# New orders of the same instructions in a fused chunked attention and snake-MLP kernel

## The chip, the cores and the metric

The kernel runs on one core of one Trainium2 chip. The metric is device time in microseconds (us), as the median of several executions. Before the change that median is 220.3 us, from three executions between 216.8 and 222.6 us. One further execution was taken by the hardware profiler; it took 214.84 us, and all times inside the kernel below come from it.

## The reference, cut to what matters

Four batches of 768 positions, eight heads of 64 channels. First a chunked attention: each chunk of 32 queries sees 16 keys to its left, its own 32, 8 to its right, and 8 memory keys. The result, 3072 rows of 512 channels, goes through a two-layer MLP of width 2048 whose activation is snake.

```
for c in range(nc):                       # 24 chunks of 32 positions
    k_full = concat(mem_k, k[c_start-16 : c_end+8])
    scores = scale * q_c @ k_full.T       # scale = 1/8
    a = softmax(scores)
    attn[c] = a @ v_full
x = attn.transpose(0, 2, 1, 3).reshape(3072, 512)
h = x @ w_in                              # 512 -> 2048
s = sin(alpha * h)
g = h + s * s / alpha
out = g @ w_out                           # 2048 -> 512, f32
```

## The kernel before, in words

The work is cut by batch. A stage runs the MLP of one batch (768 rows) on TensorE, and beside it the attention of the next batch. A front (stage -1) computes only the attention of batch 0, so five lists of words exist: the front, and passes 0, 1, 2 and 3. The last pass has no attention beside it.

Nothing is planned by a scheduler. Each list is an order written out by hand, and each word issues a few instructions. The engines run asynchronously, but each engine executes its own instructions in the order of the words; so a word moved in the list is moved on every engine and every queue that it issues to. The words, with their lines in the code:

- a (cast of a q or k piece to bf16, L653), k and l (12 TensorE transposes of a k or q piece, L274), K and L (the copy out of PSUM; for K a second small copy of the ends always on VectorE: L285, L291, L299). A trailing A means ScalarE, V means VectorE, P means GpSimd. Pieces a0 to a3 are k of head pair 0 to 3, a4 to a7 are q.
- s (scores, then exp on ScalarE: L317 to L332 for batch 0, L385 to L399 for the others), v (attention times values, L344 or L414, then the division on VectorE, L353 and L354, into a block of x).
- The block has to be turned into xT before the MLP can read it. T and t do it by four TensorE transposes (L366) and a copy out of PSUM (L369) by ScalarE or VectorE. c does it by a transposing DMA through the crossbar (L633), issued from the SP queue, with no compute engine in it.
- V (values by two or three DMAs from GpSimd's queue, L168 to L179), dm (the memory values, one DMA, L665), m (their copy into the value tile by VectorE, L188), I and U (the weights), R (rows of k and q of a coming batch, by GpSimd's queue), X (crossbar transposes of those rows, by the SP queue), Z (memory rows, SP queue), dk and dq (a whole batch of k or q).
- b and h (first layer of one of 16 feature tiles, first and second half, 4 matmuls each of 384 columns, L424; h also issues the Sin on ScalarE, L439), q (the square of the sine, L444 on ScalarE or L447 on VectorE or GpSimd), g (the sum into gT on VectorE, L451, which frees the tile's pair of PSUM banks).
- o and f (o opens the second layer of the pass, f takes n of its 96 matmuls, L462; finished rows are copied out at L469 and stored by the SP queue). In the last pass all 96 run behind the list.
- z (matmuls on zeros, L686), W (a dummy activation that brings in ScalarE's table for Exp or Sin, L699), e (which engine copies output rows), C (constants), H and Z (memory rows).

PSUM has eight banks. A feature tile holds a pair from its b to its g, a score or a value product holds a pair until it is read, and the open output rows hold one bank each. So at most four tiles are in flight, and TensorE waits at a b whose pair is not yet free. The order of the banks, of the x blocks and of the probability tiles is also decided by the order of the words.

Inputs of batch 0 come by eight DMAs from the SP queue (L708), in the order k0, q0, k1, q1, k2, q2, k3, q3.

Of the kernel before, what the change touches and what calls it, by code (L numbers as in the profile page):

```python
# [85 lines left out]
def kernel(  # L86
# [716 lines left out]
    def const_s():  # L803
# [7 lines left out]
    stage = Stage(-1, None)  # L811
    stage.tile = first
    stage.run((
# [3 lines left out]
    ))  # L817
    for i, words in enumerate(((
# [6 lines left out]
    ),(  # L825
# [5 lines left out]
    ),(  # L831
# [5 lines left out]
    ),(  # L837
# [3 lines left out]
    ))):  # L841
        stage = Stage(i, stage.nx).run(words)
    feed.take(400)
# [29 lines left out]
```

## Time and profile before

| What | us |
|---|---|
| median of three executions | 220.3 (216.8 to 222.6) |
| the profiled execution | 214.84 |
| its span, first to last instruction | 213.1 |
| TensorE (PE) busy | 201.7 (95%) |
| ScalarE (ACT) busy | 143.5 (67%) |
| VectorE (DVE) busy | 140.5 (66%) |
| GpSimd (POOL) busy, its DMA issues included | 99.8 (47%) |
| first layer, 512 matmuls (L424) | 86.0 |
| second layer, 400 matmuls (L462) | 89.1 |
| squares: ACT x30, DVE x23, POOL x11, mean of one | 0.84, 0.95, 1.58 |

A matmul is pipelined and its end is modelled, so TensorE counted as busy is not TensorE at its peak. Idle time of an engine costs something only where it holds up the engine that ends last. The chain that ended last runs 71% over PE, 9% over DVE, 7% over DMA, 4% over ACT and 3% over POOL. The granted clock of TensorE was 1.000.

### The profile page before, as it was taken

Reading aid. Unit: us, or ns where it says so; the run is one execution under the profiler, and the core shown is the slowest. Engines: PE = TensorE matmul, PEld = TensorE weight load, DVE = VectorE, ACT = ScalarE, POOL = GpSimd, SP = SyncE. Lnnn points to the kernel's source line nnn. Section 1 sums busy time; section 2 is a strip of 40 time slices with the busy share of each in tenths; the row PEclk is TensorE's granted clock in tenths of the full one; section 3 lists DMA queues with packets and bytes.
Section 4 is the critical chain, followed back from the end, with each engine's and each line's share of the span. In section 5 each row is a group of like instructions: output and inputs, shape, how many; then the busy total and the mean of one; then the engine's idle time right before and its main releaser. Section 6 shows DMA issues by size and latency. Waiting matters only on the chain.

```text
span 213.1 us, 4479 instructions
## 1 busy us (share of the span) xinstructions
PE 201.7 (95%) x1721; PEld 113.5 (53%) x1721; DVE 140.5 (66%) x218; ACT 143.5 (67%) x230; POOL 99.8 (47%) x140
## 2 busy tenths in 40 slices
PE   0799899999999999999999999999999999999994
PEld 0456555565455556555455555554555555554443
DVE  7598678999542749975856649898157197865011
ACT  2597898976857469977846199887846289891110
POOL 8959515688598193009991039659400023200000
PEclk9999999999999999999999999999999999999999
DMA  6999999999999999969999229989945400000312
GB/s 195 337 163 141 193 209 205 204 163 182 131 177 141 137 148 144 180 88 110 126 217 171 72 63 131 156 126 129 175 115 123 124 15 0 2 3 0 148 49 98
DMA packets 95908, 28.19 MB, mean 132 GB/s; under 512 B 84864, under 2 KB 92432, under 8 KB 95888
## 3 DMA queue, kind: packets, MB, share of 16 engines
q0 software_dynamic: 68736, 13.25, 92.3%
q1 hardware_dynamic: 26976, 14.62, 28.2%
q8 instruction: 13, 0.21, 0.4%
q14 instruction: 7, 0.06, 0.1%
q10 hardware_dynamic: 176, 0.04, 0.1%
HBM read 29.66 MB, written 6.29 MB: 169 GB/s over the span
## 4 chain that ended last, share of the span: by engine, by line
PE 71%; DVE 9%; DMA 7%; ACT 4%; issue 4%; POOL 3%; DVEq 0%; POOLq 0%; ACTq 0%
PE ps L462 38%; PE ps L424 27%; DMA memv_st<-in_mem_v_dram 4%; DVE gT L451 4%; DVE s L447 3%; DMA vw<-in_v_dram 3%; PE ps L414 3%; PE ps L385 2%; ACT u L439 2%; PE ps L366 1%; ACT s L444 1%; POOL s L447 1%; POOL vw L172 1%; DVE kT L285 1%; ACT L699 1%
## 5 line engine op out<-in xcount | busy, mean ns | idle before, releaser
L462 PE MATMUL ps<-w_out_sb,gT 128*128 128x512 bf16 (+2 forms) x400 | 89.1, 371 | 0.0
L424 PE MATMUL ps<-xT,w_in_sb 128*128 128x384 bf16 x512 | 86.0, 326 | 0.7 <-DVE gT L451 0.4
L451 DVE SCALAR_TENSOR_TENSOR gT<-s,inv_alpha,ps 128x768 bf16<-128x768 f32 x64 | 63.0, 1011 | 12.5 <-ACT s L444 5.2
L424 PEld LDWEIGHTS <-w_in_sb 128*128 128x128 bf16 x512 | 49.8, 98 | 35.4 <-issue 2.1
L439 ACT ACTIVATE u<-ps,alpha_sb 128x768 f32<-128x768 f32 x64 | 56.6, 895 | 16.8 <-PE ps L424 14.3
L462 PEld LDWEIGHTS <-gT 128*128 128x128 bf16 x400 | 36.6, 98 | 37.9 <-DVE gT L451 0.2
L447 POOL TENSOR_TENSOR s<-u 128x768 f32<-128x768 f32 x11 | 17.4, 1582 | 69.7 <-ACT u L439 69.7
L399 ACT ACTIVATE pt<-ps,biasm 128x256 bf16<-128x256 f32 x72 | 27.2, 489 | 10.5 <-PE ps L385 10.5
L469 DVE COPY o_sb<-ps 128x512 f32<-128x512 f32 (+1 forms) x15 | 10.1, 678 | 28.3 <-PE ps L462 26.4
L447 DVE TENSOR_TENSOR s<-u 128x768 f32<-128x768 f32 x23 | 21.9, 953 | 7.8 <-ACT u L439 7.8
L444 ACT ACTIVATE s<-u 128x768 f32<-128x768 f32 x30 | 25.0, 841 | 0.5
L354 DVE TENSOR_TENSOR x_blk<-ps,rinv 96x512 bf16<-96x512 f32 x32 | 22.0, 687 | 1.1
L469 ACT COPY o_sb<-ps 128x512 f32<-128x512 f32 (+1 forms) x10 | 5.6, 562 | 21.6 <-PE ps L462 21.6
L172 POOL DMA_DIRECT2D vw<-in_v_dram x13 | 12.9, 994 | 7.9 <-PE ps L366 5.4
L353 DVE RECIPROCAL rinv<-ps 96x8 f32<-96x8 f32 x32 | 6.4, 200 | 13.5 <-PE ps L414 12.7
L179 POOL DMA_DIRECT2D vw<-in_v_dram x13 | 12.7, 976 | 0.0
L238 POOL DMA_DIRECT2D kst<-in_k_dram x16 | 12.2, 760 | 1.1 <-DMA vw<-in_v_dram 0.8
L232 POOL DMA_DIRECT2D kst<-in_k_dram x16 | 11.3, 708 | 2.3 <-DMA vw<-in_v_dram 1.6
L369 ACT COPY xT<-ps 128x384 bf16<-128x384 bf16 x12 | 5.6, 496 | 8.2 <-PE ps L366 8.2
L245 POOL DMA_DIRECT2D q_bf<-in_q_dram x12 | 10.7, 912 | 0.0
L414 PEld LDWEIGHTS <-pt 128*128 128x128 bf16 x192 | 8.2, 97 | 4.2 <-ACT pt L399 0.3
L414 PE MATMUL ps<-vw,pt 128*128 128x65 bf16 x192 | 8.9, 193 | 0.0
(81 smaller groups left out, 131.4 us busy)
## 6 DMA issues: line engine op xcount, KB each, us to landing
out_dram<-o_sb SPq DMA_DIRECT2D x23, 256.0 KB, 2.3
kq_f<-in_k_dram SPq DMA_DIRECT2D x4, 384.0 KB, 6.5
kq_f<-in_q_dram SPq DMA_DIRECT2D x4, 384.0 KB, 6.0
q_bf<-in_q_dram POOLq DMA_DIRECT2D x12, 128.0 KB, 6.7
w_in_sb<-in_moe_w_in_dram POOLq DMA_DIRECT2D x1, 1152.0 KB, 12.6
vw<-in_v_dram POOLq DMA_DIRECT2D x7, 128.0 KB, 6.7
vw<-in_v_dram POOLq DMA_DIRECT2D x8, 112.0 KB, 7.4
kst<-in_k_dram POOLq DMA_DIRECT2D x14, 64.0 KB, 5.1
```

Of the source, the lines that this page charges most:

```text
L172: nc.gpsimd.dma_start(vw[0:64, lo:c1, 0:D], win(vflat, a, n, 64))
L179: nc.gpsimd.dma_start(vw[72:128, c0:hi, 0:D], win(vflat, base + QW * c0 + 48, hi - c0, 56))
L354: nc.vector.tensor_tensor(out=x_blk[:].rearrange("p g e d -> p e g d"), in0=otv[0:QW, :, :, 0:D], in1=rinv[:].unsqueeze(3).to_broadcast([Q ...
L399: nc.scalar.activation(pt[:, 0:H * QW].rearrange("p (g e c) -> p g e c", g=2, e=4)[:, :, :, 32 * m:32 * m + 32], sc[:, :, 0:4 * QW].rearra ...
L414: nc.tensor.matmul(otv[:, e, hp, :], pt[:, QW * i:QW * i + P], vws[b % 2][:, 2 * hp + e, j, 0:D + 1],)
L424: nc.tensor.matmul(t["hT"][:, hf, 0:HALF], w_in_sb[:, kt, P * t["ft"]:P * t["ft"] + P], t["xT"][:, kt, HALF * hf:HALF * hf + HALF], start= ...
L439: nc.scalar.activation(t["u"][:], t["hT"][:, :, 0:HALF], ACTF.Sin, scale=alpha_sb[:, ft:ft + 1])
L444: nc.scalar.activation(s2[:], u[:], ACTF.Square)
L447: e.tensor_tensor(out=s2[:], in0=u[:], in1=u[:], op=ALU.mult)
L451: nc.vector.scalar_tensor_tensor(out=gT[:, ft, :].rearrange("p (e c) -> p e c", e=2), in0=t["s2"][:], scalar=inv_alpha[:, ft:ft + 1], in1= ...
L462: nc.tensor.matmul(o[:, c0:c1], gT[:, ft, P * s:P * s + P], w_out_sb[:, ft, c0:c1], start=(ft == 0), stop=(ft == FT - 1),)
L469: copier(state["engines"][state["o"] % len(state["engines"])])(o_sb[:, c0:c1], o[:, c0:c1])
```

## The change

All five lists are written in another order. The number of instructions stays nearly the same; what changes in kind is this:

- Front: of the casts, a4 and a6 go from VectorE to ScalarE; of the copies out of PSUM, L1 goes to ScalarE, K1 to VectorE and K2 to ScalarE; two turned x blocks (30 and 31) go from ScalarE to VectorE. dm moves behind V024 in GpSimd's queue. The first four zero matmuls stand at the head. The first score word comes behind L1, a6 and K2 instead of ahead of a3.
- Pass 0: the square of tile 14 goes from VectorE to GpSimd, with V102 moved behind it; blocks 1 and 7 are copied by VectorE instead of ScalarE; block 3 goes through the crossbar and block 4 by TensorE instead of the other way round.
- Pass 1: the square of tile 7 goes from VectorE to GpSimd, that of tile 14 from ScalarE to VectorE; blocks 0 and 1 go through the crossbar instead of TensorE (five crossbar blocks instead of three); 5 and 6 exchange their copying engines. The dummy Exp comes behind the first scores.
- Pass 2: order only.
- Pass 3: the square of tile 14 goes from ScalarE to GpSimd.

The removed (-) and added (+) lines of the front and of passes 0, 1 and 3, cut to these places:

```diff
-        'a1A Cb Cp Cz Cv a5A eVA Cm Cl z4 a0V Ci k0 dm a4V l0 k1 K0V Ck l1 L0A V024 We L1V a2A K1A V002 '
-        'a6V k2 s00 K2V a3V s11 V068 m0 a7V s01 l2 s10 k3 K3A L2A V046 z4 v10 l3 Cs L3A I02 v11 s20 z1 '
-        'v01 s30 z1 v00 s31 z1 v30 s21 v31 T01 T10 v20 T30 T00 v21 T20 T31 I27 t11 t21 eVA Ws '
+        'Cz Cb a1A z4 a0V eVA Cp Cl k0 a4A a5A Cv Ck Ci l0 L0A K0V Cm l1 V024 a2A dm k1 V002 We k2 L1A K1V '
+        'a6A K2A a3V V068 s01 l2 m0 s00 a7V s10 s11 k3 K3A z4 L2A l3 L3A v10 Cs V046 v11 I02 z1 s30 v00 s20 '
+        'v01 s31 v30 s21 z1 T10 v31 z1 t30 T01 v20 v21 T00 t11 T20 t31 Ws eVA I27 t21 '
...
-        'o8 b0 h0 I7g q0V U69 U12 b1 h1 dq108 q1A b4 h4 b3 g0 h3 b6 g1 dk108 q4V g4 q3A b2 h2 h6 b5 h5 '
+        'b0 h0 o8 q0V I7g b1 U12 h1 U69 q1A dq108 g0 b4 dk108 h4 g1 b3 h3 b6 b2 q4V g4 q3A U56 h2 h6 b5 h5 '
...
-        'q15V h12 q12A b14 g15 f7 h14 V125 k1 k0 g12 l1 K1V k3 L1V L3A q14V K3A K0A V102 f9 g14 s61 f16 '
-        'm1 s70 s3 f13 v0 f3 v6 c6 f6 v3 f5 s542 T3 f10 T0 v4 f6 v2 f2 v1 c4 c2 f7 v7 f1 T1 f3 v5 Ws T7 '
-        'f8 t5 '
+        'q12A b14 f5 h14 g12 V125 k1 k0 l1 k3 K1V L1V L3A f2 q14P K3A K0A f9 g14 s61 f16 V102 s70 s3 m1 f13 '
+        'v0 f2 v3 f6 c3 v6 c6 f5 s542 f10 T0 v4 f8 v1 t4 v2 c2 v7 f7 t1 Ws f4 v5 f8 t7 f1 t5 '
...
-        'h15 f7 eV We s24 q15V f6 g15 f7 V268 s05 s1 f1 m2 f14 v4 v1 f6 v0 f1 v2 f2 c4 f6 s63 s7 t1 f4 c2 '
-        'v6 V357 T0 f4 v3 f4 v7 c7 v5 t3 f17 t5 T6 '
+        'q11A g7 f10 Ws b12 h12 g10 g11 q12P b14 g12 h14 b13 h13 q13A V202 q14V f7 X6 g13 b15 h15 f7 g14 s24 '
+        'q15V eV g15 f13 m2 s1 We V268 s05 f15 v4 v0 c4 v1 f6 v2 c2 f9 s63 s7 c1 f4 v6 V357 f4 v3 f4 v7 c0 v5 '
+        'c7 f3 t3 f14 t6 T5 '
...
-        'g12 b13 h13 b14 q15A h14 g15 q14A q13V g14 g13 '
+        'b14 g12 q13V q15A h14 q14P g13 g14 g15 '
```

23 rows, old and new, of the table stage are left out of this document.

## The prediction

> **What bounds the kernel now.** I read the page's busy shares first, then the busy time of each stage, then the front in order of time, then the chain.
>
> ```profile
> PE 201.7 (95%) x1721; PEld 113.5 (53%) x1721; DVE 140.5 (66%) x218; ACT 143.5 (67%) x230; POOL 99.8 (47%) x140
> PE   0799899999999999999999999999999999999994
> ```
>
> TensorE is nearly always busy, but not in the first slices. The table by stage (columns: length, then busy time of each engine with its instructions) has the front, passes 0, 1, 2, and pass 3 with the tail:
>
> ```profile
> 0.00:24.80 24.80, 17.19 (x289) 11.45 (x290) 19.54 (x54) 15.80 (x24) 21.00 (x50) 1.00 1.82 206
> 24.80:75.60 50.80, 50.30 (x473) 28.68 (x471) 35.53 (x52) 38.34 (x64) 30.79 (x38) 1.00 1.60 174
> 75.60:121.90 46.30, 46.29 (x370) 25.45 (x368) 33.34 (x47) 32.51 (x57) 22.18 (x27) 1.00 1.57 139
> 121.90:168.30 46.40, 46.24 (x362) 25.26 (x359) 30.18 (x42) 34.04 (x57) 21.37 (x23) 1.00 1.15 123
> 168.30:213.10 44.80, 41.72 (x240) 22.71 (x238) 21.88 (x24) 22.83 (x30) 4.44 (x3) 1.00 0.13 48
> ```
>
> From 24.8 us on TensorE is the bound: it idles 0.50, 0.01 and 0.16 us in three passes. Short waits hide in matmuls whose ends are modelled, so I also took the starts: a first-layer matmul follows the last after 162 ns at the median, a second-layer one after 216. All spacings over their line's median by more than 60 ns, without the roughly 0.1 us paid at each change to the 64-row score matmuls and back, add up to 2.9 us behind 24.8 us. That is all a better order can win in four passes, beside instructions that vanish. The front is the other place: 24.8 us in which TensorE waits for others.
>
> ```profile
> 7.30 0.83 ACT L653 CAST k_bf<-kq_f 128x768 bf16<-128x768 f32 x1 [3.87 <-DMA kq_f<-in_k_dram]
> 12.31 3.04 ACT L332 ACTIVATE pt<-ps 128x768 bf16<-128x768 f32 x4 [0.45 <-PE ps L325]
> 14.45 1.22 DVE L188 COPY vw<-memv_st 8x4096 bf16<-8x4096 bf16 x1
> 17.09 0.80 ACT L299 COPY qT<-ps 128x768 bf16<-128x768 bf16 x1 [0.43 <-PE ps L274]
> 24.81 11.91 PE L424 MATMUL ps<-xT,w_in_sb 128*128 128x384 bf16 x69
> 26.45 0.88 ACT L439 ACTIVATE u<-ps,alpha_sb 128x768 f32<-128x768 f32 x1
> ```
>
> ScalarE starts at 7.30, when k1 lands; its first four exps run from 12.31, its last q copy ends at 17.89, the MLP begins at 24.81 and the first Sin at 26.45. The chain shows what else stands there (start, length):
>
> ```profile
> 4.86 9.20 DMA memv_st<-in_mem_v_dram
> ...
> 14.34 1.75 POOL vw L172
> 16.09 6.06 DMA vw<-in_v_dram
> ```
>
> GpSimd's loads land in the order of issue, about 9 us behind it while the input loads are under way: memv from 4.86 at 14.06, V024 from 5.75 and 6.57 at 14.97 and 15.97.
>
> **The front, step by step.** In the new order ScalarE does, from 7.30: a1, a4, a5 (0.83 each), L0 (0.80), a2, the dummy (0.20), L1, a6 and K2 (0.70) before any exp. a4's input has landed at 5.8 (1.26 plus 4.5), yet it queues behind a1. 7.30 + 5 x 0.83 + 2 x 0.80 + 0.20 + 0.70 = 13.95: the first exp is 1.6 us later than 12.31. Four exps of 0.81, then K3, L2, L3 (0.70 + 2 x 0.80) end at 19.5, against 17.89. The next scores need L3: 0.65 on TensorE, then four exps of 0.81, about 23.5, against 21.99.
>
> VectorE loses a4, a6, L1 and K2 and gains K1 and two block copies, 1.5 us less work by their rows. But dm is now the third of GpSimd's loads: issued about 6.7, it lands near 15.9, where the third landed before (15.97), instead of 14.06. m0 waits for it on VectorE, with a7 and the ends of K3 queued behind it, and everything after a7 (l3, L3, v10) for those. m0 ends at 17.2 (before 15.67); a7 (0.6) 17.8; l3 stands ahead of v10 on TensorE, so the first division starts near 19.0 (before 16.56). Six more divisions of 0.89 lie ahead of block 20's end with one block copy of 0.4: 19.0 + 7 x 0.89 + 0.4 = 25.6. Its transposes (0.35) and T20 (0.43) give the first b at 26.4. Had memv landed in time, v31's exp would hold block 20 to about 25.2 and b to 26.0. t21 ends near 27.5, against 25.4, and h0 needs it. So the front costs **+1.6 us**, bounds +0.6 (divisions never queue, the two block copies taken from ScalarE pay) and +2.3 (Sin 28.5 against 26.45, with its table load behind T20). Nothing in pass 0 absorbs it: the weights it needs land at 26.72 and 32.17 and are not waited for.
>
> The zero matmuls now run near 1 us instead of 6.28, followed by idle until the alpha rows land at 5.96. Before, the four took 1.89 us, and 12 transposes 0.85 at 8.10 but 0.53 from 10.7 on.
> The Trainium skill, TensorE: Matmul & The Clock Gate, Part 1, says that the array runs at half rate until about 3.4 us of sustained work and falls back after an idle window as long. The halving agrees with these rows; by it the early zeros would be wasted and one more set of turns cold, 0.3 us, an estimate, and the front +1.9 instead of +1.6.
>
> **Pass 0.** Its end is where VectorE is late:
>
> ```profile
> 52.18 0.95 DVE L447 TENSOR_TENSOR s<-u 128x768 f32<-128x768 f32 x1
> 53.04 0.41 DVE L291 COPY kT<-ps 128x96 bf16<-128x96 bf16 x2
> 53.52 0.51 PE L385 MATMUL ps<-qT,kT 64*128 64x96 bf16 x16 [0.20 <-DVE kT L291]
> ```
>
> The 0.95 us square of tile 14 stands ahead of the key ends that the first scores wait for. On GpSimd it takes 1.46 to 2.03; V125 is issued by 49.3, so it can run from 50.7, and g14 is due about 4.8 us behind h14 against 0.9 + 1.8 + 1.0. The wait (0.36 from the starts) goes: **-0.4**, bounds -0.8 (with the three smaller waits of 44 to 51) and +0.5 (square and division late). V102 and the row loads move back by up to 3.2 us; its heads landed at 58.7 for a use at 61.1, and the row loads had 5.4 us of idle behind them. Late by more, v0 is next.
>
> **Pass 1.** Two blocks fewer on TensorE: 8 transposes at 42 ns start to start, **-0.3**. The copies (0.5 and 0.35) lie beside 0.216 us matmuls of the second layer. q7 on GpSimd: its loads ahead are issued by 81.7, it is free till 96.06, and it spares VectorE 0.95 off the path. The added crossbar blocks share SP's queue:
>
> ```profile
> 110.55 1.50 SPq L633 DMA_TRANSPOSE xT<-x_blk  x1
> 114.05 5.99 SPq L633 DMA_TRANSPOSE xT<-x_blk  x2
> ```
>
> One is 1.2 to 1.5 us in SP's queue and landed after 2.3 us (from 118.86) or 6.1 (from 110.55, among GpSimd's loads). Two more fit before block 7's if each takes the short time: c0 near 119, c7 near 120.2, landed by 122.5; b3 starts at 122.1 and h0 at 123.4. I take 0; the bound is +3.0, the long landing (120.2 + 6.1 = 126.3 against 123.4). The other bound is 0: that landing is not waited for now. The dummy Exp behind the scores puts 1.28 of table load ahead of the exps; 13 matmuls (2.8 us) cover it.
>
> **Passes 2 and 3** keep their work. Their waits were 1.1 us by the starts; an order can remove or double them, so 0, bounds -1.1 and +1.1. In pass 3, g14 is needed 28 second-layer matmuls (6.0 us) behind h14, and 0.9 + 1.8 + 2.0 fits; without this cover 1.0 us of the slower square would show.
> In the new lists three squares more go to GpSimd; at 133.73 one took 2.03 us beside VectorE's own square, at 126.04 1.46 almost without.
> The Trainium skill, GPSIMD Engine Reference, its specification table, says that GpSimd contends with VectorE instructions that read two SBUF inputs. The rows agree (VectorE's square stays 0.95); by it each new square costs 0.6 more at most, all covered, and the sum stays.
>
> **Sum.** +1.6 - 0.4 - 0.3 = +0.9: 215.7 us for the profiled execution's 214.84 (span 213.1, 1.7 around it). The median of the runs shown lies 5.5 above that execution, so **221.2 us** stands for the median, 220.3 + 0.9.
>
> **Rivals.**
> - *The passes win, the front is neutral.* Half of the 2.9 us of waits and the transposes: -1.8, 218.5. For it: ScalarE was busy 14.5 of the 17.5 us between 7.3 and 24.8 (15.80 less the 1.28 table load before), gaps which a denser order can use. Against it: the first exp waits for five casts and copies more. Chance 0.22.
> - *Slower: the crossbar blocks of pass 1 land late.* c0 or c7 behind V357's loads takes 6.1 us instead of 2.3, and TensorE stands before h0 of pass 2 for 3.0 us; with the front 1.6, +4.6: 224.9. It decides once c7 lands after 123.4 in the old clock. For it: 6.1 and 6.3 us landings at 110.55 and 98.86. Against it: 2.3 at 118.86, when those loads were through. Chance 0.13.
> - *It does nothing that counts.* TensorE runs the same matmuls, and the loads, not the casts, set the front (V046 landed 22.15, TensorE waited 0.25 for it): 220.3. Chance 0.10.
>
> **How the numbers follow.** Forecast 0.55 (its bounds: +0.6 - 0.8 - 0.3 - 1.1 = -1.6 and +2.3 + 0.5 - 0.3 + 1.1 = +3.6, or 218.7 to 223.9). 2%, 4.4 us, is about what a measurement of this kernel can tell from no change; three runs alone lay 5.8 apart. Slower by over 2%: the crossbar case nearly whole and a few hundredths of the forecast's upper end, 0.14. Faster by over 2%: no sum reaches it, since 2.9 + 0.3 is the limit of the passes; 0.06 for a front that gains on top. The rest 0.80. The range takes in 218.5 less the spread of medians, and 224.9.
>
> **What would show it.** First exp near 14.0 and first L424 near 26.4; L188 starting near 16 with a wait on memv_st; at the first L385 of pass 0 no wait on kT; L366 x64 instead of x72 and L633's xT x16; no wait on xT at the turn to pass 2. Wrong, if the first b comes by 24.8, or if TensorE's waits behind the front change by more than 2 us.

## The result and the profile after

The new orders cost time: 218.22 us is the median of 20 executions (216.3 to 220.8), against 215.48 us for 20 of the kernel before, a ratio of **1.0113 [1.0083, 1.0143]**, about 2.4 us. That is inside the 2% that the prediction called no difference, but it is a loss, and nearly three times the +0.9 us of the forecast. The three executions shown at first (216.8, 220.3, 222.6) lay high, so 220.3 was a poor base: 218.22 lies below the forecast's bounds of 218.7 to 223.9, and the same bounds counted from 215.48 are 213.9 to 219.1. Ratios, not medians, are compared from here on.

The profiled execution of the changed kernel took 219.58 us (span 217.4). It is one of 4 in 20 with a granted clock of 0.991 or 0.992 over the span (those four took 218.7 to 220.8 us); in its trace the clock is at half for 3.4 us of the front, so the trace shows more loss (4.7 us) than the median does. The page's busy line, TensorE's slices and its granted clock:

```profile
PE 201.9 (93%) x1694; PEld 114.5 (53%) x1713; DVE 138.8 (64%) x218; ACT 141.6 (65%) x225; POOL 104.7 (48%) x143
PE   3495989999999999999999999999999999999994
PEclk9998899999999999999999999999999999999999
```

TensorE is busy as long as before (201.9 against 201.7 us) in a span 4.3 us longer, and the idle slices are the first ones. The same table by stage as before (front, passes 0, 1, 2, then pass 3 with the tail):

```profile
0.00:29.08 29.08, 18.78 (x287) 12.76 (x290) 18.03 (x52) 17.41 (x26) 21.08 (x51) 0.94 1.58 193
29.08:80.00 50.92, 50.10 (x470) 28.81 (x473) 35.69 (x55) 36.94 (x60) 32.80 (x40) 1.00 1.59 160
80.00:126.00 46.00, 45.62 (x359) 25.10 (x363) 32.84 (x47) 31.18 (x55) 23.48 (x27) 1.00 1.59 149
126.00:172.60 46.60, 46.08 (x354) 25.35 (x356) 30.46 (x43) 34.05 (x57) 21.43 (x23) 1.00 1.22 122
172.60:217.40 44.80, 41.32 (x237) 22.47 (x236) 21.80 (x24) 22.02 (x29) 5.91 (x4) 1.00 0.12 46
```

The front is 29.08 us instead of 24.80: TensorE waits 10.30 us in it instead of 7.61, and is busy for 18.78 instead of 17.19, at a granted clock of 0.94. Cut at the first L424 of each pass, the four passes take 50.54, 46.36, 46.16 and 20.97 us (to the last L424 of pass 3); before 50.67, 46.58, 46.08 and 21.01. So they are 0.31 us shorter together. From the start of the last matmul to the end of the span it is 3.44 us, before 3.05. 4.27 - 0.31 + 0.39 = 4.35 us is the span's difference. The front in order of time (start, length, engine, line, and in brackets the wait and what ended it):

```profile
7.97 0.83 ACT L653 CAST k_bf<-kq_f 128x768 bf16<-128x768 f32 x1 [4.55 <-DMA kq_f<-in_k_dram]
...
14.03 2.87 ACT L332 ACTIVATE pt<-ps 128x768 bf16<-128x768 f32 x4
...
17.35 1.22 DVE L188 COPY vw<-memv_st 8x4096 bf16<-8x4096 bf16 x1 [2.46 <-DMA memv_st<-in_mem_v_dram]
18.60 0.75 DVE L653 CAST q_bf<-kq_f 128x768 bf16<-128x768 f32 x1
...
19.40 0.73 PE L274 MATMUL ps<-ident,q_bf 128*64 128x128 bf16 x12 [2.59 <-DVE q_bf L653]
...
20.73 0.20 DVE L353 RECIPROCAL rinv<-ps 96x8 f32<-96x8 f32 x1 [1.22 <-PE ps L344]
...
23.42 2.41 ACT L332 ACTIVATE pt<-ps 128x768 bf16<-128x768 f32 x3 [0.26 <-PE ps L325]
...
29.08 5.20 PE L424 MATMUL ps<-xT,w_in_sb 128*128 128x384 bf16 x31
...
30.58 0.90 ACT L439 ACTIVATE u<-ps,alpha_sb 128x768 f32<-128x768 f32 x1 [0.30 <-PE ps L424]
```

One queue after another is to be seen here. VectorE stands 2.46 us at m0 (L188) for the memory values; a7, the cast of the last q piece, stands behind it and ends at 19.35; TensorE stands 2.59 us at l3 for a7, with the first value product behind. Before, m0 ran at 14.45 with no wait. From l3 the chain to the first L424 runs through the copy L3 and the scores to the last three exps, which end at 25.83, and then through three divisions (L353, L354). k1 landed 0.67 us later in this execution (7.97 against 7.30); in the other traces it lands between 6.77 and 8.70, by chance. The chain has the load itself (start, length):

```profile
7.05 10.27 DMA memv_st<-in_mem_v_dram
```

Here 32 KB need 10.27 us, where the prediction took 9.2. The Trainium skill, DMA: Bandwidth & Descriptors, Anatomy of one DMA (the GpSimd path), gives a fit of 2.0 us plus bytes over 436,000 per us for one such DMA, an estimate of 2.1 us for this one; the trace does not agree with it under this load. That the loads ahead in the queue and the input loads beside it make the difference is argued from the order of the landings.

### The profile page after: what moved, and what is told of

Read it like the earlier page. It is cut to its first block, busy times and chain, and to the rows that moved or that the text cites. A ratio compares the mean times of both kernels' runs of the same rounds, so it can differ in the third digit from the quotient of the medians.

```text
span 217.4 us, 4445 instructions
## 1 busy us (share of the span) xinstructions
PE 201.9 (93%) x1694; PEld 114.5 (53%) x1713; DVE 138.8 (64%) x218; ACT 141.6 (65%) x225; POOL 104.7 (48%) x143
## 4 chain that ended last, share of the span: by engine, by line
PE 74%; DVE 10%; DMA 5%; ACT 4%; issue 4%; POOL 3%; DVEq 0%; POOLq 0%
PE ps L462 38%; PE ps L424 27%; DVE gT L451 5%; DMA memv_st<-in_mem_v_dram 5%; PE ps L414 3%; DVE s L447 2%; PE ps L385 2%; ACT u L439 1%; ACT s L444 1%; ACT pt L332 1%; PE ps L274 1%; DVE x_blk L354 1%; PE ps L366 1%; PE ps L344 1%; DVE vw L188 1%
## 5 line engine op out<-in xcount | busy, mean ns | idle before, releaser
L462 PE MATMUL ps<-w_out_sb,gT 128*128 128x512 bf16 (+2 forms) x383 | 87.0, 370 | 1.2 <-issue 0.5
L424 PE MATMUL ps<-xT,w_in_sb 128*128 128x384 bf16 x512 | 86.0, 326 | 0.8 <-DVE gT L451 0.5
L424 PEld LDWEIGHTS <-w_in_sb 128*128 128x128 bf16 x512 | 49.8, 98 | 35.4 <-issue 2.0
L447 POOL TENSOR_TENSOR s<-u 128x768 f32<-128x768 f32 x14 | 21.7, 1551 | 79.0 <-ACT u L439 42.7
L447 DVE TENSOR_TENSOR s<-u 128x768 f32<-128x768 f32 x22 | 21.0, 957 | 8.8 <-ACT u L439 8.8
L444 ACT ACTIVATE s<-u 128x768 f32<-128x768 f32 x28 | 23.5, 841 | 0.7
L354 DVE TENSOR_TENSOR x_blk<-ps,rinv 96x512 bf16<-96x512 f32 x32 | 22.0, 687 | 1.1
L353 DVE RECIPROCAL rinv<-ps 96x8 f32<-96x8 f32 x32 | 6.3, 198 | 15.6 <-PE ps L414 13.5
L232 POOL DMA_DIRECT2D kst<-in_k_dram x16 | 12.8, 798 | 0.0
L238 POOL DMA_DIRECT2D kst<-in_k_dram x16 | 11.6, 727 | 0.0
L245 POOL DMA_DIRECT2D q_bf<-in_q_dram x12 | 10.8, 914 | 0.0
L274 PE MATMUL ps<-ident,q_bf 128*64 128x128 bf16 x96 | 4.8, 252 | 4.8 <-DVE q_bf L653 2.6
```

The costliest lines, as they stand in the source:

```text
L232: nc.gpsimd.dma_start(kst[r0:64, j, :].rearrange("p (h d) -> p h d", d=D), k[b, :, lo + r0:lo + 64, :].rearrange("h p d -> p h d"),)
L354: nc.vector.tensor_tensor(out=x_blk[:].rearrange("p g e d -> p e g d"), in0=otv[0:QW, :, :, 0:D], in1=rinv[:].unsqueeze(3).to_broadcast([Q ...
L424: nc.tensor.matmul(t["hT"][:, hf, 0:HALF], w_in_sb[:, kt, P * t["ft"]:P * t["ft"] + P], t["xT"][:, kt, HALF * hf:HALF * hf + HALF], start= ...
L444: nc.scalar.activation(s2[:], u[:], ACTF.Square)
L447: e.tensor_tensor(out=s2[:], in0=u[:], in1=u[:], op=ALU.mult)
L462: nc.tensor.matmul(o[:, c0:c1], gT[:, ft, P * s:P * s + P], w_out_sb[:, ft, c0:c1], start=(ft == 0), stop=(ft == FT - 1),)
```

## The experiments

In the tables "front" is the first L424 less the landing of k1, which takes the luck of the input load out; before it is 17.5 us, after 21.1. One trace has some 0.5 us of chance in this (the seven traces with the front of before, those of before, e2, e11 and e15 to e18, lie between 16.8 and 17.8), so a ratio, where there is one, decides.

### One half each

e1 has the front of after and the passes of before; e2 the front of before and the passes of after.

```diff
-        'a1A Cb Cp Cz Cv a5A eVA Cm Cl z4 a0V Ci k0 dm a4V l0 k1 K0V Ck l1 L0A V024 We L1V a2A K1A V002 '
...
+        'Cz Cb a1A z4 a0V eVA Cp Cl k0 a4A a5A Cv Ck Ci l0 L0A K0V Cm l1 V024 a2A dm k1 V002 We k2 L1A K1V '
...
```

> The front in the new order, all four passes in the old one. Theory (the front lost it): as slow as the changed kernel, +2.0 to +2.8 us on the kernel before, first L424 at 27 to 29 us. Rival (the passes lost it, by their squares and crossbar blocks): within 0.5 us of the kernel before.

```diff
-        'o8 b0 h0 I7g q0V U69 U12 b1 h1 dq108 q1A b4 h4 b3 g0 h3 b6 g1 dk108 q4V g4 q3A b2 h2 h6 b5 h5 '
...
+        'b0 h0 o8 q0V I7g b1 U12 h1 U69 q1A dq108 g0 b4 dk108 h4 g1 b3 h3 b6 b2 q4V g4 q3A U56 h2 h6 b5 h5 '
...
```

> The front in the old order, all four passes in the new one. Theory (the front lost it, the passes win little): between -0.7 and +0.3 us on the kernel before, first L424 near 24.8. Rival (the passes lost it): +2 us or more.

| Kernel | Ratio to before | front | passes 0, 1, 2, 3 | tail |
|---|---|---|---|---|
| e1, new front | 1.0089 [1.0055, 1.0124] | 20.2 | 50.56, 46.59, 46.07, 21.02 | 3.05 |
| e2, new passes | 1.0025 [0.9998, 1.0052] | 17.4 | 51.43, 46.36, 46.17, 20.97 | 3.45 |

The front is worth +1.9 us (1.2 to 2.7 by its interval) and the passes +0.5, at whose lower end nothing is lost; together they make the 2.4. The passes won nothing, though the prediction gave them -0.7. In e2's trace pass 0 is 0.76 us longer than before, by this wait a little behind its start (TensorE in order of time):

```profile
25.01 2.77 PE L424 MATMUL ps<-xT,w_in_sb 128*128 128x384 bf16 x16
28.58 1.64 PE L424 MATMUL ps<-xT,w_in_sb 128*128 128x384 bf16 x9 [0.81 <-DMA w_in_sb<-in_moe_w_in_dram]
```

A piece of the first weights is late when the front is not: in this execution the MLP could not have run on before 28.5 whatever the front did.

### The front: which of its edits costs

The prediction had two parts in the front's step: five casts and copies more on ScalarE ahead of the first exp (by themselves the first b at 26.0), and m0 waiting for a third load, with a7 and l3 behind (the first b at 26.4). These kernels start from after. e3 gives dm its place ahead of V024 again:

```diff
-l1 V024 a2A dm k1
+l1 dm V024 a2A k1
```

> The changed kernel with dm put back ahead of V024 in GpSimd's queue. Theory A (m0's wait on memv, with a7, l3 and v10 behind it, is most of the front's loss): m0 starts near 15, first L424 near 26, 1.5 to 3 us faster than the changed kernel. Theory B (the casts and copies moved to ScalarE are most of it): within 0.5 us of the changed kernel, as the exps stay late.

e4 puts the casts and copies back on their engines and leaves the load where it is:

```diff
-a4A ... L1A K1V a6A K2A
+a4V ... L1V K1A a6V K2V
```

> The changed kernel with a4, a6, L1, K1 and K2 back on the engines that had them before, dm still third. Theory A (m0's wait on memv is most of the loss): the first exp comes 1.5 us sooner, but m0 still starts near 16 to 17 and the first L424 stays within 0.7 us of the changed kernel. Theory B (the casts on ScalarE are most of it): 1 to 2 us faster than the changed kernel.

e6 does both, the edits of e3 and e4:

> The changed kernel with dm ahead of V024 and also the casts and copies back on their old engines. If the casts count once memv is in time: first exp near 13, first L424 1 us or more sooner than with dm alone, the time within 0.3 us of the new passes behind the old front (+0.5 us on the kernel before). If they never count: the same as with dm alone (+0.9 us).

e7 leaves the load late and takes a7 out from behind m0:

```diff
-l2 m0 s00 a7V s10
+l2 a7V m0 s00 s10
```

> The changed kernel with a7 ahead of m0 on VectorE, dm still third. If the wait on memv costs by what is queued behind it (a7, so l3, L3 and the second four exps): l3 3 us sooner, the time 0.8 to 1.5 us below the changed kernel. If it costs by the divisions alone, which need m0: within 0.4 us of the changed kernel.

| Kernel | Ratio to before | front | m0 starts (its wait) |
|---|---|---|---|
| after | 1.0113 [1.0083, 1.0143] | 21.1 | 17.35 (2.46) |
| e4, casts back | 1.0113 [1.0080, 1.0146] | 20.8 | 16.71 (2.12) |
| e3, dm first | 1.0042 [1.0019, 1.0065] | 18.4 | 15.64 |
| e6, both | 1.0074 [1.0041, 1.0108] | 17.4 | 14.24 |
| e7, a7 ahead of m0 | 1.0070 [1.0041, 1.0099] | 18.4 | 16.45 |

In e4 the first exp starts at 13.14, 0.9 us earlier than in after, and the time does not change, since m0 still waits for memv (timeline of e4: m0, l3, first L424):

```profile
16.71 1.22 DVE L188 COPY vw<-memv_st 8x4096 bf16<-8x4096 bf16 x1 [2.12 <-DMA memv_st<-in_mem_v_dram]
...
18.77 0.53 PE L274 MATMUL ps<-ident,q_bf 128*64 128x128 bf16 x12 [2.34 <-DVE q_bf L653]
...
28.41 1.79 PE L424 MATMUL ps<-xT,w_in_sb 128*128 128x384 bf16 x10
```

So the casts are hidden as long as m0 waits, and the first exp is not what sets the front then. dm's place takes back 0.7% (1.5 us), a7's place 0.4% (0.9 us, with an interval that overlaps after's). Whether the casts cost something once the wait is gone stays open: e6's trace has a front 1.0 us shorter than e3's, but its ratio is not lower. Of its trace's gain 0.9 us went at the end, where its last two stores landed 1.81 and 2.54 us behind the last copy, against 1.36 and 1.63 in after.

### The clock in the front

The half clock is the other thing that after's front shows. In the table by stretch of after's TensorE (length, busy times, then the granted clock as third number from the end) it follows a sparse stretch:

```profile
12.70:19.50 6.80, 3.92 (x76) 2.42 (x74) 3.39 (x7) 5.51 (x9) 3.15 (x4) 1.00 3.37 115
19.50:23.00 3.50, 3.50 (x49) 2.39 (x51) 1.73 (x6) 1.45 (x2) 3.50 (x6) 0.51 1.35 121
```

TensorE was busy for 3.92 of 6.80 us, a stretch with the 2.59 us wait in it, and then ran at 0.51 for 3.5 us. The Trainium skill, TensorE: Matmul & The Clock Gate, Part 1, lets the clock fall after an idle window of about 3.4 us and return after one of sustained work. The length of the half clock agrees; a whole idle window is not in the trace, only a stretch of that kind. e5 fills the stretch with eight zero matmuls more, from the kernel after:

```diff
-z4 L2A l3
+z4 L2A z8 l3
```

> The changed kernel with eight more zero matmuls (1.7 us) in TensorE's idle 2.6 us between the last early transposes and l3. Theory (the idle stretch lets the clock of TensorE fall back to half, which costs 1 to 1.6 us in the executions where it does): no half-clock stretch in the profile, granted clock 0.999 or more, the median 0.3 to 0.8 us below the changed kernel. Rival (the cold stretch lies beside VectorE's divisions and costs nothing): the same time as the changed kernel.

Measured 1.0124 [1.0076, 1.0173], with the granted clock at 1.00 through the whole front and a front of 19.8 us. The clock stayed up and the time did not fall below after's 1.0113, so e5 shows no part of the loss that is the clock's; its six executions would still allow 0.8 us. The four executions of after with the lower clock have a median of 219.5 us, the other 16 one of 218.1: whether the half clock costs this, or a longer wait that brings it, stays open.

### The same edits in the old front

If dm's place is the cause, dm third in the front of before should cost the same. e9 moves it, from the kernel before:

```diff
-k0 dm a4V
+k0 a4V
...
-L0A V024 We
+L0A V024 dm We
```

> The kernel before with one word moved: dm behind V024 in GpSimd's queue, nothing else. Theory (the load order by itself costs, through m0's wait): m0 starts near 16 to 17 instead of 14.5, first L424 1 to 2 us later, +1.0 to +1.8 us on the kernel before. Rival (it costs only together with the rest of the new front): within 0.4 us.

1.0031 [1.0002, 1.0060]: 0.7 us, m0 at 16.46 after a wait of 2.38, front 18.5. It costs, but by the ratios half of the 1.5 us that it costs in the new order, though the wait on VectorE is as long. In both lists a7 and l3 stand behind m0; in the old one the first value product (v10) stands ahead of l3 and goes without a7. Whether that makes the difference was not tested.

e8 asks the opposite, whether the loads can be had sooner: dm and V024 go near the head of GpSimd's queue, from the kernel before.

```diff
-Cb Cp Cz Cv a5A
+Cb Cz dm V024 a5A
...
-k0 dm a4V
+k0 a4V
...
-L0A V024 We
+L0A V002 Cp We
-K1A V002 a6V
+K1A a6V
-V068 m0
+V068 Cv m0
```

> The kernel before, in its old order, with GpSimd's constants moved behind its first loads: dm and V024 issued from about 2.5 instead of 4.9 us, the others near 2 us sooner too. If the landing of the values sets the old front: memv lands near 12, first L424 1 to 2 us sooner, 0.5 to 1.5 us faster than the kernel before. If the DMA engines are full with the inputs anyway: memv lands near 14 again and the time is within 0.4 us of the kernel before.

1.0035 [1.0006, 1.0065], a loss. memv, issued at 2.30, landed at 10.72 instead of 14.06; but V024, issued 2.5 us sooner, landed at 15.11 against 14.97 before. An earlier issue moved the small load and not the large one.

### The front mended

e10 has the front of after with both mends, dm first and a7 ahead of m0, and the old passes (its expectation speaks of the new passes; the kernel that ran kept the old ones).

```diff
-l1 V024 a2A dm k1
+l1 dm V024 a2A k1
...
-l2 m0 s00 a7V s10
+l2 a7V m0 s00 s10
```

> The new front with dm first and a7 ahead of m0, and the new passes. Theory (the wait on memv and what it holds up are the whole loss of the front): within 0.3 us of the new passes behind the old front, that is +0.2 to +0.8 us on the kernel before. Rival (something else in the new front costs as well): +0.9 us or more, as with dm alone.

0.9998 [0.9973, 1.0023], against e1's 1.0089. Its front in order of time (a7, m0, l3, first L424):

```profile
15.25 0.54 DVE L653 CAST q_bf<-kq_f 128x768 bf16<-128x768 f32 x1
...
15.82 1.22 DVE L188 COPY vw<-memv_st 8x4096 bf16<-8x4096 bf16 x1
...
17.01 0.53 PE L274 MATMUL ps<-ident,q_bf 128*64 128x128 bf16 x12
...
26.07 4.23 PE L424 MATMUL ps<-xT,w_in_sb 128*128 128x384 bf16 x25
```

No wait is left at m0 or l3, k1 landed at 8.24 and the front took 17.8. By the ratios the loss of the new front is these two places, and the rest of its new order, the casts among it, is worth between -0.6 and +0.5 us. The traces say more: e10, and e13 and e14 below with the same front, have the first L424 at 26.07, 26.15 and 26.16 (front 17.8, 18.7, 18.4), against 24.59 to 25.40 in the seven with the old front, and the chain of e10 runs through ScalarE's casts and copies. So the casts still set a later first b; why the time shows so little of it is open. Some of a shorter front is given back in pass 0, where TensorE waits for the first weights in e2, e16 and e17 (0.97, 0.99 and 0.36 us by the starts).

### The passes: crossbar blocks

e13 has both mends of the front with the new passes; e14 is e13 with blocks 0 and 1 of pass 1 back on TensorE; e11 is e2 with the same two blocks back; e15 is the kernel before with those two blocks through the crossbar, and nothing else.

> The changed kernel with dm ahead of V024 and a7 ahead of m0: mended front, all passes new. If the new passes cost 0.5 us by themselves: +0.3 to +0.8 us on the kernel before. If they cost nothing: within 0.2 us of it.

e14 and e11 have, in pass 1 of after's list:

```diff
-s7 c1 f4
+s7 t1 f4
...
-v7 c0 v5
+v7 T0 v5
```

> The same mended front and the new passes, with blocks 0 and 1 of pass 1 turned by TensorE again. If the two crossbar blocks are what the new passes cost: 0.4 to 0.9 us faster than with them, equal to the kernel before or up to 0.5 us faster. If not: the same as with them.

> The old front and the new passes, with blocks 0 and 1 of pass 1 turned by TensorE again instead of the crossbar. If two more crossbar DMAs cost by moving the last stores to other semaphores: the tail behind the last matmul 0.39 us shorter than in the new passes, pass 1 longer by the 0.34 us of eight transposes, the sum the same. If they cost by late landings or in the DMA engines: faster than the new passes by 0.3 us or more.

e15 has, in pass 1 of before's list:

```diff
-s7 t1 f4
+s7 c1 f4
...
-V357 T0 f4
+V357 c0 f4
```

> The kernel before with blocks 0 and 1 of pass 1 by the crossbar in place of TensorE, nothing else. If the crossbar blocks cost: +0.3 to +0.9 us, the tail behind the last matmul 0.39 us longer, pass 1 about 0.2 us shorter. If their tail and the spared transposes only cancel: within 0.2 us.

| Kernel | Ratio to before | pass 1 | tail |
|---|---|---|---|
| e13, front mended, new passes | 1.0032 [1.0002, 1.0062] | 47.85 | 3.44 |
| e14, the same, two blocks back | 1.0008 [0.9984, 1.0031] | 46.54 | 3.05 |
| e2, old front, new passes | 1.0025 [0.9998, 1.0052] | 46.36 | 3.45 |
| e11, the same, two blocks back | 0.9984 [0.9953, 1.0015] | 46.53 | 3.06 |
| e15, before with two crossbar blocks | 0.9983 [0.9963, 1.0003] | 46.42 | 3.65 |

In the new order the kernels without the two blocks are better by 0.24% and 0.41%; in the old order they are better by 0.17% with them. The intervals of each pair overlap, and e15's holds 1, so the sign of the two blocks is not settled. What the traces do show has two sides. The eight transposes saved make pass 1 shorter by 0.16 to 0.22 us (46.58 to 46.36 or 46.42). Against it the tail is 0.4 to 0.6 us longer in the kernels with the two blocks (the last of the experiments).

In e13 pass 1 has a wait which the prediction did not think of: not at the turn to pass 2, where the new blocks are, but at the second set of scores. The same wait stands in e7 (TensorE in order of time, first e13, then e7):

```profile
104.66 0.35 PE L385 MATMUL ps<-qT,kT 64*128 64x96 bf16 x8 [1.31 <-DVE gT L451]
```

```profile
104.75 0.35 PE L385 MATMUL ps<-qT,kT 64*128 64x96 bf16 x8 [1.13 <-DMA qT<-q_bf]
```

e7's line names the crossbar DMA of q. In e13 the line names VectorE, but TensorE's queue stood on the semaphore of the fourth of those DMAs until 104.55, three hundredths behind its signal, and in e14 the same scores go at 103.2 with the same gT on VectorE running from 103.60 to 104.61, with no wait: the releaser named is the wrong one. The two added blocks stand behind these scores in the list, so they are not the cause of the wait either. What differs is where SP's crossbar transposes of k begin, ahead of those of q: 4.2 us behind the store of the memory rows (L253) in the kernel before, 4.6 in after, 4.9 in e14, 5.7 in e7 and 6.2 in e13. Up to 5.1 (e5) no trace has a wait there; at 5.7 and more all have. What moves it is not settled. The length of pass 1 in e13's row is this wait, of one execution.

### The passes: squares

The new lists move the square of tile 14 to GpSimd in passes 0 and 3, and in pass 1 that of tile 7 to GpSimd and that of tile 14 from ScalarE to VectorE. e16 makes these four moves in the lists of before; e17 only that of pass 0; e18 only the two of pass 1.

```diff
-q14V
+q14P
...
-q7V
+q7P
-q14A
+q14V
...
-q14A
+q14P
```

> The kernel before with the four squares of the change on their new engines (tile 14 of pass 0, tile 7 of pass 1 and tile 14 of pass 3 to GpSimd, tile 14 of pass 1 to VectorE), in the old order. My theory: the 0.36 us wait of the first scores of pass 0 goes, all else is covered, -0.3 us, within what can be measured of no change. Rival (the slower GpSimd squares hold up banks): passes 1 or 3 longer by 0.3 us or more.

> The kernel before with one edit: the square of tile 14 of pass 0 on GpSimd. If the loads queued behind it are the cost: V102 issued near 52.8 instead of 49.3, the last row and q loads and the crossbar transposes of them 1 to 3 us later, TensorE waiting on xT or qT near 76 or 102, +0.8 to +1.8 us. If my prediction's term holds: -0.4 us.

> The kernel before with two edits in pass 1: the square of tile 7 on GpSimd, that of tile 14 on VectorE. If the loads behind the square of pass 0 are the cost: within 0.3 us of the kernel before. If the slower square holds a bank pair, or the square on VectorE delays the last tiles: +0.5 us or more, pass 1 longer.

| Kernel | Ratio to before | pass 0 | pass 1 |
|---|---|---|---|
| e16, all four | 1.0083 [1.0055, 1.0111] | 51.65 | 47.37 |
| e17, pass 0 | 1.0015 [0.9975, 1.0055] | 51.82 | 46.53 |
| e18, pass 1 | 1.0044 [1.0011, 1.0077] | 50.64 | 47.41 |

The moves of pass 1 cost 0.8 us in the old order, because q14 now stands on VectorE ahead of the sums that free the banks (e18 in order of time: the square of tile 14, its sum g14, and the two waits; the waits in brackets are short since a matmul's end is modelled, and by the starts TensorE loses 0.41 us at each of the two places):

```profile
100.56 0.95 DVE L447 TENSOR_TENSOR s<-u 128x768 f32<-128x768 f32 x1
...
101.55 1.01 DVE L451 SCALAR_TENSOR_TENSOR gT<-s,inv_alpha,ps 128x768 bf16<-128x768 f32 x1
...
102.62 0.35 PE L385 MATMUL ps<-qT,kT 64*128 64x96 bf16 x8 [0.23 <-DVE gT L451]
...
104.61 1.69 PE L462 MATMUL ps<-w_out_sb,gT 128*128 128x512 bf16 x7 [0.24 <-DVE gT L451]
```

The new order of pass 1 has the same squares on the same engines and a pass of 46.36 us. There q14 stands ahead of g13 on VectorE, where in e18 it stands behind it, and runs while ScalarE still squares tile 13; the two sums follow without a wait (after):

```profile
102.52 0.95 DVE L447 TENSOR_TENSOR s<-u 128x768 f32<-128x768 f32 x1
...
103.52 1.94 DVE L451 SCALAR_TENSOR_TENSOR gT<-s,inv_alpha,ps 128x768 bf16<-128x768 f32 x2
```

So the new order pays for the squares; pass 1 is then shorter by the transposes and no more.

In pass 0 the wait of the first scores on the key ends is gone in e17, as foreseen. But its trace gives back, by the starts, 0.88 us at 55.53 on weights of the second layer, 0.36 at 28.27 on those of the first and 0.31 at 77.13 on xT; the ratio tells no difference. In after the kT wait is gone too, and a b waits 0.34 us, by the starts, for a sum on VectorE instead:

```profile
51.24 0.81 PE L424 MATMUL ps<-xT,w_in_sb 128*128 128x384 bf16 x4 [0.18 <-DVE gT L451]
```
In e16, 0.99 us of pass 0's length is the wait for w_in at 27.03 that e2 also has, and 0.42 a wait on a crossbar block at 75.78; the V102 loads, which stand behind the square on GpSimd, were issued at 52.80 instead of 49.29.

### The tail

The new kernel has two more DMAs in SP's queue than the old one, and its tail is 0.39 us longer. At the end SP looks at the semaphores of its DMAs one after another, 0.06 us each, in a fixed order, and the DMAs use these semaphores in turn. Before, the last two stores are on the last two looked at: seven others are looked at while the stores fly. After, they are on the second and third: six looks, 6 x 0.06 = 0.37 us, come behind their landing. To test it, e12 is the kernel before with two more DMAs, one output store of pass 0 being cut in three:

```diff
-            nc.sync.dma_start(out[S * i + P * s:S * i + P * s + P, c0:c1], o_sb[:, c0:c1])
+            cuts = [0, 128, 256, d_model] if (i, s) == (0, NSUB - 1) else [c0, c1]
+            for ca, cb in zip(cuts, cuts[1:]):
+                nc.sync.dma_start(out[S * i + P * s:S * i + P * s + P, ca:cb], o_sb[:, ca:cb])
```

> The kernel before, with one output store of pass 0 cut into three DMAs of the same rows, so that SP issues two DMAs more. If the position of the last stores in SP's ring of semaphores sets the length of the tail: last matmul to end 3.4 us instead of 3.05, +0.4 us, the passes unchanged. If not: tail 3.05, no difference.

The tail was 3.42, as after's; e11 and e14, with the two blocks back and so two DMAs fewer, have 3.06 and 3.05. The count of DMAs shows in the tail, then, with the flight of the last stores on top (4.34 and 4.35 in e4 and e6). But the whole kernel came to 1.0303 [1.0256, 1.0349], a loss of 6.5 us that no step of ours holds. Its pass 1 took 53.67 us (TensorE at its scores):

```profile
105.71 0.50 PE L385 MATMUL ps<-qT,kT 64*128 64x96 bf16 x8 [3.08 <-DMA qT<-q_bf]
...
107.36 0.50 PE L385 MATMUL ps<-qT,kT 64*128 64x96 bf16 x8 [1.15 <-DMA qT<-q_bf]
```

SP's crossbar transposes of k in pass 1 begin 7.2 us behind the store of the memory rows, at 85.42 instead of 80.76 with a first L424 only 0.5 us later, and those of q behind them at 96.93 instead of 91.58. TensorE waits 4.2 us for them, and its clock is at half for 6.8 us behind that. Why the k transposes begin so late is not settled; all six executions (221.6 to 229.9 us) show that this one edit of pass 0 is that dear.

## Where the prediction was right, and where it was wrong

The step that failed is the passes' -0.7 us: by e2 the new passes cost +0.5 us ([0.9998, 1.0052]), since a wait removed in pass 0 gave nothing and the two added DMAs lengthen the end of the kernel by 0.39 us, a term that the prediction did not have. In after's trace the four passes win 0.31 us and the end gives 0.39 back; in e2's, where the front is early, the wait for the first weights comes on top.

- **What bounds the kernel**: right. TensorE is the bound behind the front; its busy time did not change, and most of the loss is in the front.
- **The front, +1.6**: right in its mechanism and near in size, 1.9 us by e1. e1's trace follows the working: m0 starts at 16.29 (15.9 foreseen), the first division at 19.27 (19.0), the first b comes at 26.92 (26.4). The wait of m0 for memv with a7 and l3 behind it is shown by e3, e7 and e10. In after all is later, m0 at 17.35, since the load was issued at 7.05 instead of 6.7 and took 10.27 us instead of 9.2; from l3 on the second four exps set the pace, not the queue of divisions. What the working put too low is the share of the load's lateness: it moves the first b only from 26.0 to 26.4, and by e3 dm's place is worth 1.5 us. With memv in time the first b does stand at 26.07 to 26.16, as foreseen, but e10's time shows at most 0.5 us of that. The first exp came at 14.03 for 13.95, in part by luck: k1 landed 0.67 us later than assumed, and ScalarE's casts follow one another after 0.73 us, not 0.83 (7.97, 8.71).
- **The cold clock, 0.3 us by the Trainium skill, TensorE: Matmul & The Clock Gate, Part 1**: the rows behave as it says. Twelve transposes still take 0.85 us at 10.59, where before they took 0.53 from 10.71. No time of its own was seen; e5, which tests a later half clock, shows none.
- **Pass 0, -0.4**: the wait of the first scores on kT went, as foreseen. What failed is the step from "the wait goes" to "-0.4". The stage is 0.13 us shorter in after, and e1, with the old pass 0 behind the new front, has nearly the same (50.56 against 50.54), so the new order is worth 0.02. The wait at 51.24 took the old one's place; with the old front, e2 and e17 wait for weights.
- **Pass 1, -0.3**: the stage is 0.22 us shorter, near the 8 x 42 ns. The term missed two prices. q14's move from ScalarE to VectorE was never costed, only q7's: 0.8 us in the old order, which the new order has to win back. And each added DMA was costed in SP's queue at the turn to pass 2 only, not at the end of the kernel, where the two cost 0.39 us.
- **Passes 2 and 3, 0**: right, +0.08 and -0.04 us.
- **The sum, +0.9 against +2.4**: the front is 0.3 more, and the passes are +0.5 for -0.7. The 221.2 us lies 3 us over the measured 218.2, because the base of 220.3 was the median of three high executions, 4.8 us over 215.48. That error went the other way from the change, which was forecast too small.
- **The rivals**: the front is not neutral (e1), so the first fell. The crossbar case with its wait at the turn to pass 2 did not come: TensorE begins pass 2 at 125.98 without a wait on xT, c7 being through by then. The chain of DMAs that is in truth just in time is the one of q in the middle of pass 1 (waits of 1.13 us in e7, 1.3 in e13, 4.2 in e12). That the change does nothing fell too, by the interval.

No version here is clearly faster than the kernel before: the nearest are e15 at 0.9983 [0.9963, 1.0003] and e11 at 0.9984 [0.9953, 1.0015].

## What to carry to other kernels

A load that lands in the order of issue costs what stands behind its reader, not what it is: ask for each reader which instructions of its engine wait behind it, and move those ahead or the load forward (here 0.9 and 1.5 us). When work goes from one engine to another, price it on both ends, and for each DMA look at every later use of its queue, the end of the program among them. Three times here (after, e2, e17) an order without the kT wait met another wait in pass 0, so a term for a wait removed is worth only as much as the slack of what is late next.

## What was not expected of the hardware

- GpSimd's loads beside the input loads land in order 8.6 to 10.8 us behind their issue (before and after); issued 2.5 us sooner (e8), the small one came 3.3 us sooner and the larger one no sooner.
- The end of the program depends on how many DMAs a queue has carried: 3.05 us of tail or 3.44, by the place of the last stores among the semaphores that SP looks at.
- One output store of pass 0 cut into three DMAs (e12) made pass 1 7.1 us longer.
- A zero-filled gap kept TensorE's clock at 1.00 (e5) without any gain in the median.
